# Re-ordering a fused attention and feed-forward kernel by a searched list, with its last up projection as seven block products

## The chip, the cores and the metric

The kernel runs on one core of a Trainium2 chip. The time is the device time of one execution in microseconds (us). Most executions of one kernel agree within a few tenths of a per cent. An execution is called slow when it is over 1.5% above the fastest of the same kernel. The engines are named as in the profile: PE is TensorE, PEld its weight loads, DVE is VectorE, ACT is ScalarE, POOL is GpSimd, and SP issues most transfers.

## The reference, cut to what matters

Four batches of eight heads with 768 tokens of width 64 go through an attention in which a token sees only the tokens of its own cluster. The result, 3072 tokens of width 512, goes through a feed-forward layer with exact GELU.

```
q_assign = argmax(q/|q| . c/|c|)          # 16 centroids per head; k the same
scores   = where(q_assign == k_assign, q @ k.T / 8, -1e9)
x        = (softmax(scores) @ v)          # -> (3072, 512)
h        = x @ w_in                       # 512 -> 2048, the "up projection"
out      = gelu(h) @ w_out                # 2048 -> 512, the "down projection"
```

## The kernel before

The kernel is a list of small operations. Each has an engine, an estimated duration, a due date, what it depends on and which buffers it takes. A greedy planner simulates the engines with assumed durations and orders the operations. The instructions of each engine then run in that order, so an engine whose next instruction has to wait stands, whatever is behind it.

```python
class Plan:
    def run(self):
        ...                                  # for each engine: the ready operation
        key = (t, op.due)                    # that can start first, then by due date
        ...
order = plan.run()
for op in order:
    op.emit()
```

The up projection of half a batch is 64 operations of two matmuls each, and eight full-width gelus:

```python
for m in (2 * half, 2 * half + 1):           # four of these per "hp" tile
    nc.tensor.matmul(T["hp", hb, fp][:, e, 0:QB],
                     w_in_sb[:, m, f * 128:(f + 1) * 128],
                     T["xt", b][:, m, t * QB:(t + 1) * QB],
                     start=(m == 0), stop=(m == NM - 1))
```

The down projection of a batch was already a 2x2 split with seven block products (of the Strassen-Winograd kind). It needs sums of the gelu outputs, called S1 to S4 here. Each is 128x768 in f16, there are 64 of them in the four batches, and all run on VectorE:

```python
def sums(k_, fs=fs):
    ...
    if k_ == 1:
        nc.vector.tensor_add(s1, a21, a22)
    else:
        sub(*{2: (s2, s1, a11), 3: (a21, a11, a21), 4: (a12, a12, s2)}[k_])   # nc.vector.tensor_sub
```

The k and q of a head are split into two f16 pieces, a tile called `st` of which three buffers exist. From head 8 on, `st` is transposed by a transfer (`dtr8`, `dtr9` and so on, tile `kqT`). TensorE then multiplies the result by the centroids, the "assignment" (`asn`).

The softmax here doesn't subtract the row's maximum and nothing guards it: scores larger than these inputs give would overflow.

Of the kernel before, what the change touches and what calls it, by code (L numbers as in the profile page):

```python
# [8 lines left out]
FP32 = mybir.dt.float32  # L9
# [10 lines left out]
    "0a 0b 1a 1b 2a 3a 4a 5a 2b 6a 7a 4b 5b 3b f0 6b 7b 8a 8b f1 9a 9b 10a 10b 11a "  # L20
# [5 lines left out]
SHIFT = dict((w.rsplit("=", 1)[0], int(w.rsplit("=", 1)[1])) for w in (  # L26
    "fc2_2_P6_0_1=41 fc2_0_P1_1_1=20 fc2_0_P2_0_1=18 fc2_0_P5_0_0=33 fc2_0_P5_0_1=6 "
    "fc2_0_P4_0_0=19 fc2_0_P3_0_1=21 fc2_0_P5_1_0=21 fc2_0_P7_1_1=23 fc2_0_P3_1_1=9 "
    "fc2_0_P4_1_0=21 fc2_0_P6_2_1=21 fc2_0_P5_2_1=21 fc2_0_P3_2_0=21 fc2_0_P4_2_0=33 "
    "fc2_1_P1_0_0=9 fc2_1_P2_1_0=33 fc2_1_P1_2_0=15 fc2_1_P6_0_0=23 fc2_1_P6_0_1=17 "  # L30
    "fc2_1_P7_0_0=9 fc2_1_P7_0_1=21 fc2_1_P5_0_0=14 fc2_1_P4_0_1=15 fc2_1_P6_1_0=22 "
    "fc2_1_P4_1_0=21 fc2_1_P6_2_1=24 fc2_1_P5_2_0=20 fc2_1_P5_2_1=22 fc2_1_P7_2_1=24 "
    "fc2_1_P3_2_0=35 fc2_1_P4_2_0=19 fc2_1_P4_2_1=16 fc2_2_P1_1_1=36 fc2_2_P2_1_1=-1 "
    "fc2_2_P1_2_0=18 fc2_2_P7_0_1=33 fc2_2_P4_0_0=33 fc2_2_P5_1_0=21 fc2_2_P7_1_1=21 "
    "fc2_2_P3_1_0=24 fc2_2_P3_1_1=6 fc2_2_P4_1_0=13 fc2_2_P6_2_1=18 fc2_2_P5_2_0=12 "
    "fc2_2_P7_2_1=21 fc2_2_P4_2_0=26 fc2_3_P1_0_0=21 fc2_3_P1_0_1=21 fc2_3_P1_1_0=23 "
    "fc2_3_P1_1_1=19 fc2_3_P5_0_1=22 fc2_3_P7_1_1=13 fc2_3_P3_2_1=21 fc1_4_0_3=-9 "
    "fc1_4_1_3=7 fc1_4_3_1=-9 fc1_6_6_3=-15 fc1_2_7_3=11 fc1_5_3_3=-2 fc1_6_3_2=-2 ge2=6 "
    "norm9_1=2 sc22a1=7 fc2_0_P1_2_0=18 fc2_0_P6_1_0=18 fc2_0_P6_2_0=18 fc2_0_P4_2_1=18 "
    "fc2_2_P1_1_0=18 fc2_2_P6_0_0=6 fc2_2_P5_0_0=27 fc2_3_P2_0_1=21 u30_3=-26 exp13b1=-64 "  # L40
    "exp13b2=-54 asnk30=-18 ge28=-1 S3_10=12 av29b1=17 exp12b1=-23 exp30b1=-36 exp2a2=14 "
    "exp4a1=26 exp2b0=17 exp2b2=26 exp5a0=29 exp5a1=19 exp6a0=-4 exp6a2=2 exp5b0=32 "
    "exp5b1=21 exp6b2=-11 sc4a2=27 evq0=10 fc1_0_1_3=24 fc1_0_7_0=-2 fc1_3_5_2=6 "
    "sc15a1=-8 sc15b0=-10 sc15b1=-9 dtr30=27 c221_0=-11 c221_3=-26 sc24a1=-20 sc24a2=-28 "
    "sc24b2=-21 ge27=-3 hik8=-3 stc1112=8 av6a0=42 av6a1=40 av6b0=41 loadv20=8 hik6=3 "
    "c211_1=11 fc2_0_P5_2_0=1 fc2_1_P1_0_1=-10 fc2_1_P1_1_1=9 fc2_1_P4_0_0=8 "
    "fc2_2_P6_1_0=1 fc2_2_P5_1_1=7 fc2_3_P7_2_1=1 gelu7_0=-3 sc2b0=-37 sc2b1=-38 "
    "sc2b2=-40 rec7_0=3 exp20b2=16 exp8a0=20 exp8b0=2 ohd24=2 putk7=8 evk1=5 t1_2=2 "
    "fold11=-5 fc1_0_6_0=13 fc1_5_7_2=13 fc1_6_5_3=19 av11a0=21 rec28_1=-11 sc29a2=-42 "
    "sc3b2=39 sc18a2=-10 v11=8 c110_1=-7 S2_32=-10 av10a2=10 av10b1=8 av10b2=-7 av11a1=20 "  # L50
    "av11b0=15 av12a1=10 av12a2=11 norm8_1=9 c222_1=16 c222_3=18 exp18a1=-39 exp18b2=-47 "
    "putk28=20 ohd16=11 gelu7_7=-2 ge31=-2 av2b1=23 exp22a0=5 exp22b0=11 exp23b2=-59 "
    "av7a0=47 exp31a2=14 asnq25=-11 loadv1=-4 u22_0=28 u22_1=26 u22_2=26 v17=14 ssq=3 "
    "exp24a1=-26 exp24b1=-30 exp25b1=-37 exp28a0=3 exp28b0=6 exp28b2=-14 rec3_1=-12 "
    "putk4=-15 gelu2_3=-10 av7a2=47 av7b2=45 putk15=-12 exp19a0=-33 exp19a2=-21 putq18=22 "
    "sc28a1=-20 exp11a0=-34 exp11a1=-34 exp12a1=-22 exp14a2=-72 exp14b0=-66 exp14b1=-64 "
    "exp15a0=-29 exp15b2=-24 exp16a1=-14 exp17a0=-1 ohd12=5 asnq19=-6 S4_00=10 loadq17=8 "
    "gelu0_4=30 gelu1_0=-3 gelu1_7=-12 gelu2_1=-34 gelu2_4=-20 gelu2_5=-25 gelu2_6=-8 "
    "gelu3_0=27 exp29a0=-16 exp29b0=-16 norm3_0=6 norm3_1=-10 S3_02=-13 sc28b0=-18 "
    "sc28b1=-17 u31_0=-23 exp17a2=1 av8a1=9 sc6b0=-16 p50_0=-17 p50_2=-4 p51_2=6 "  # L60
    "av15a1=-10 rec8_1=-3 fc1_6_4_0=-3 stc2211=-15 putq4=-11 hik24=6 hik26=6 stc1120=6 "
    "v1=-11 sc29b0=-27 c210_3=11 fc2_2_P1_0_1=5 asnk12=-1 sc0a2=-19 p11_3=-6 loadk27=-1 "
    "fev020=14 exp29a1=-37 exp28a1=-3 av27b1=-1 exp24a2=-29 amax11=-3 t2_3=-1 lok12=-3 "
    "av26b0=6 S3_20=2 hiq24=13 loadv18=-14 sc25a1=-18 stc2220=16 av31a0=-2 av31a2=7 "
    "av31b1=-7 av31b2=-15 sc9a0=-5 sc9a1=14 sc9b1=2 c120_1=-16 av16a0=22 p12_0=-17 "
    "p12_3=-15 asnk24=-1 asnk20=22 rec2_0=-10 amax17=-6 av3a0=51 av3a2=51 av3b2=51 "
    "hik14=-8 hik15=-8 exp12b2=-20 fin021=28 gelu7_3=1 exp1b2=-8 dtr13=-3 lok31=-25 "
    "norm6_0=15 norm7_0=1 norm12_1=-6 sc7b2=-5 av3b1=43 sc28a2=-12 sc28b2=-9 sc30a1=-12 "
    "sc30a2=-12 sc30b0=-12 sc30b1=-13 sc30b2=-24 v8=1 S4_22=2 av22b2=28 ge23=-3 v26=-16 "
    "av12b1=8 u31_2=-15 v10=10 av27b0=-2 sc6a1=-20 sc6b1=-13 rec15_1=1 fev130=-6 loq8=1 "  # L70
    "loadv29=-4 S1_12=-15 dfin10=4 av12a0=6 fin011=-5 hiq4=8 exp10a0=35 av7b0=51 av8a0=11 "
    "av8a2=5 av8b1=6 av8b2=7 av9a0=4 av9a1=4 sc10a1=-25 sc10b0=-32 sc10b1=-27 sc11a0=-9 "
    "sc11a1=-26 sc11b0=-27 sc14b1=7 sc14b2=6 evq3=-4 hiq16=-4 sc4a0=26 sc5a0=18 sc5a2=13 "
    "sc4b1=34 asnk9=6 asnk16=20 asnq15=-1 evq4=16 c120_2=-9 evk7=-3 asnk8=-13 stc1211=-29 "
    "hiq3=-1 loadk24=6 gelu1_3=13 gelu1_4=13 gelu4_0=40 gelu4_5=39 gelu6_1=12 gelu6_2=25 "
    "gelu6_3=12 gelu6_5=-1 fold16=-1 sc17a2=-4 sc17b0=-9 loadv28=8 hik30=8 av26a0=3 "
    "av28a1=16 av28a2=-16 loadv15=1 rec26_1=-4 S1_32=-19 sc16a0=-14 sc16a1=-12 sc16a2=-9 "
    "sc16b1=-2 loadk13=-8 av1b1=13 sc31b1=-10 sc31b2=-21 asnq5=2 asnq6=12 ge29=23 "
    "av23a2=-17 av23b2=-24 sc7a0=-15 sc7b1=1 exp12a2=-21 ohtr1=-6 u20_3=-13 rec7_1=-21 "
    "ohtr4=-6 asnk31=-1 ge6=-27 asnk25=5 exp11b0=-16 rec17_1=-5 exp16b2=-9 gelu0_3=52 "  # L80
    "asnq10=12 loadv22=-5 loadv23=-10 loadv24=-15 putq10=7 putq12=-3 putq13=6 amax18=5 "
    "S4_13=1 loadq6=-5 amax19=-7 exp7b2=16 exp3b0=-12 fc1_4_1_1=-2 fc1_1_1_2=-2 loadq2=-1 "
    "putq8=-3 loq31=2 c121_3=-33 rec0_0=-8 c211_3=28 sc2a1=-35 fc1_0_5_1=-4 hik27=15 "
    "fc1_7_5_2=-11 exp26b0=3 sc19a1=-9 ohd20=-10 fin230=2 loq24=20 putq23=-5 putq9=-8 "
    "u32_1=17 trk0=3 ge8=2 exp14a1=-53 exp15b1=-10 amax4=-8 fc2_1_P2_0_1=1 exp30a1=-23 "
    "fc1_4_6_0=6 putk20=1 putk22=17 fc1_0_4_3=10 exp17a1=7 exp17b1=1 exp20a2=-5 "
    "exp22b2=36 exp30a0=-11 exp31b2=6 amax1=-7 evq1=8 ge11=-5 loadk5=7 sc23a0=-7 "
    "sc23a2=-6 sc23b1=-7 fc1_0_3_2=-4 fc1_0_4_1=-3 fc1_2_0_3=-30 fc1_2_5_2=16 "
    "fc1_2_6_0=-5 fc1_2_6_1=-13 fc1_3_4_0=11 fc1_3_5_0=7 fc1_3_7_0=7 fc1_4_0_1=-13 "
    "fc1_4_2_2=-22 fc1_4_4_2=-3 fc1_4_4_3=-6 fc1_4_7_0=-7 fc1_5_5_3=-24 fc1_5_6_0=20 "  # L90
    "fc1_6_3_1=20 fc1_6_6_0=-14 fc1_7_0_0=14 fc1_7_0_1=-3 putk31=3 sc3a0=34 sc3a2=36 "
    "exp3a0=7 exp3a2=-1 exp5a2=13 exp3b1=-4 loq16=-19 gelu6_7=15 stc2120=5 sc0a1=1 "
    "sc8a0=-5 sc8b1=-5 sc8b2=-8 loadq8=-12 av25a1=11 ge22=-15 stc2213=5 av24b0=-6 "
    "c111_3=5 fold23=17 hiq26=8 S3_21=3 rec22_1=22 norm20_1=-4 norm21_1=9 S4_10=13 "
    "S3_30=3 fc2_0_P2_1_1=2 fc2_0_P2_2_1=1 fc2_0_P7_0_0=13 fc2_0_P5_1_1=8 fc2_1_P1_2_1=-5 "
    "fc2_1_P6_1_1=-2 fc2_2_P1_0_0=8 fc2_2_P5_0_1=2 fc2_2_P4_0_1=-8 fc2_2_P6_2_0=8 "
    "fc2_3_P1_2_0=-5 fc2_3_P4_2_1=12 gelu0_1=17 gelu0_2=32 gelu0_7=34 fin130=12 "
    "sc25b1=-12 sc25b2=-12 sc9a2=-3 sc9b0=-3 sc9b2=-9 av13a2=-8 putk12=-14 av0b0=-4 "
    "exp29a2=-21 av30b2=12 amax16=5 S4_31=-2 av23a0=-6 t4_0=13 dtr12=4 asnq26=-12 "
    "sc17b1=13 S2_03=-2 gelu7_4=33 lok30=-6 exp28b1=8 loadq15=-22 norm15_1=4 sc5b2=4 "  # L100
    "sc8a2=-10 sc11b1=-13 lok27=-5 t3_1=-9 cn=-13 ohd26=9 ohd28=1 ohd30=-6 norm5_0=18 "
    "asnk3=-17 v29=-21 stc1220=11 putk3=3 hiq23=6 hiq27=12 hiq29=9 hiq30=24 S3_33=34 "
    "exp23a0=-42 exp23b0=-38 stc2221=-16 trq5=1 exp3b2=-15 sc27b1=-1 sc27b2=-18 amax2=3 "
# [150 lines left out]
class Slot:  # L254
# [3 lines left out]
    def __init__(self, pool):  # L258
        self.pool, self.users, self.place = pool, [], None
# [974 lines left out]
```

## Time and profile before

| | before |
|---|---|
| time, median of 3 runs (lowest to highest) | 302.88 us (301.42 to 303.34) |
| span of the profiled run | 301.1 us |
| first score product, first up projection | 13.95, 51.78 us |
| start of the last two up projections | 257.83 us |
| 128x768 f16 sum on VectorE, mean of each of its four groups | 563 to 622 ns |

The prediction shows the totals, the stages and the dear groups. The list of waits of TensorE has in its columns who waited, for what, how many us in all, how many times, and the longest:

```profile
PE sc_ps L844 <- ACT p_sb L853: 2.8, 7, 0.6
PE sc_ps L844 <- DVE kqT L791: 1.6, 3, 0.7
PE warm_ps L436 <- DVE half L465: 1.5, 1, 1.5
PE x_ps L881 <- DVE x_tok L908: 1.1, 3, 0.4
PE op L1125 <- DVE S L1015: 0.8, 1, 0.8
```

In the whole run TensorE stands 1.2 us for sums of the down projection (0.8 in the last line, and 0.4 in a line of the same kind, for tile `g`, that is not shown). These are the groups on VectorE that will change or, just as tellingly, not change (busy us in all, mean ns of one):

```profile
L703 DVE TENSOR_REDUCE asb<-asn_ps 128x192 f32<-128x384 f32 x24 | 13.3, 555 | 13.1 <-PE asn_ps L687 12.9
...
L791 DVE TENSOR_SCALAR kqT<-ohT 16x768 f16<-16x768 f16 x24 | 11.6, 482 | 7.6 <-DMA ohT<-oh 7.1
...
L1015 DVE TENSOR_TENSOR S<-S,g 128x768 f16<-128x768 f16 x16 | 9.1, 570 | 0.3
L1051 DVE TENSOR_TENSOR S<-g 128x768 f16<-128x768 f16 x16 | 9.0, 563 | 27.4 <-ACT g L997 27.4
...
L718 DVE TENSOR_REDUCE amax<-asb 128x12 f32<-128x192 f32 x24 | 8.4, 351 | 0.6
```

And the first transposes of `st` by transfer, issued between 30 and 60 us, from issue to landing:

```profile
DMA to landing us min/median/max: 3.8/4.4/6.2
```

### The profile page before, as it was taken

The numbers are of one execution on the slowest core, as the hardware profiler recorded it, in microseconds if no ns is written. First come the engines' busy times: TensorE is split into PE (matmuls) and PEld (weight loads), VectorE is DVE, ScalarE is ACT, GpSimd is POOL, SyncE is SP. The second block draws the span as 40 slices with busy tenths as digits, with TensorE's granted clock in tenths as the row PEclk, the third lists the DMA queues.
The fourth block names the chain that finished last, engine by engine and source line by source line (L and its number), as shares of the span: only waits on it lengthen the run. The fifth ranks groups of instructions, "written<-read, shape, count | busy, mean of one in ns | idle before, by whom it ended". The sixth has DMA issues, their size and how long they took to land.

```text
span 301.1 us, 8247 instructions
## 1 busy us (share of the span) xinstructions
PE 287.6 (96%) x3388; PEld 212.5 (71%) x3388; DVE 186.4 (62%) x432; ACT 216.3 (72%) x278; POOL 120.6 (40%) x192
## 2 busy tenths in 40 slices
PE   7899878999989999999999999999999999999995
PEld 3577655677657878866677787866678788656874
DVE  3479879966598665752676866762556553206663
ACT  5488699679689988986689778976589998366100
POOL 6989529866521976484005826620000000000020
PEclk9999999999999999999999999999999999999999
DMA  7999995998849998989229969811027312100123
GB/s 258 308 241 239 291 204 135 201 221 160 222 126 134 230 217 195 244 194 254 80 39 196 175 148 212 141 45 27 0 63 123 89 31 70 53 2 0 37 70 106
DMA packets 78038, 43.50 MB, mean 144 GB/s; under 512 B 57008, under 2 KB 77488, under 8 KB 78000
## 3 DMA queue, kind: packets, MB, share of 16 engines
q1 hardware_dynamic: 75024, 38.55, 55.7%
q0 software_dynamic: 2688, 4.19, 7.8%
q8 instruction: 26, 0.43, 0.6%
q10 hardware_dynamic: 288, 0.23, 0.2%
q14 instruction: 12, 0.10, 0.1%
HBM read 27.30 MB, written 6.29 MB: 112 GB/s over the span
## 4 chain that ended last, share of the span: by engine, by line
PE 81%; DVE 10%; ACT 5%; issue 1%; DMA 1%; POOL 0%; ACTq 0%; DVEq 0%
PE hp L983 25%; PE op L1125 22%; PE sc_ps L844 17%; PE x_ps L881 10%; ACT p_sb L853 5%; PE asn_ps L687 2%; DVE g L1015 2%; DVE kqT L791 2%; DVE kqT L788 1%; PE tr_ps L642 1%; DMA cent_sb<-in_centroids_dram 1%; PE both_ps L642 1%; DVE S L1015 1%; DVE S L1051 1%; PE warm_ps L436 1%
## 5 line engine op out<-in xcount | busy, mean ns | idle before, releaser
L853 ACT ACTIVATE p_sb<-sc_ps 128x768 f16<-128x768 f32 x192 | 146.5, 809 | 20.9 <-PE sc_ps L844 18.1
L844 PE MATMUL sc_ps<-kqT 80*128 80x384 f16 x384 | 92.3, 325 | 4.6 <-ACT p_sb L853 2.8
L983 PE MATMUL hp<-xt,w_in_sb 128*128 128x384 f16 x512 | 85.9, 326 | 0.0
L997 ACT ACTIVATE g<-hp 128x768 f16<-128x768 f32 x64 | 51.8, 811 | 35.4 <-PE hp L983 35.2
L983 PEld LDWEIGHTS <-w_in_sb 128*128 128x128 f16 x512 | 49.2, 98 | 31.4 <-issue 0.3
L881 PEld LDWEIGHTS <-p_sb 128*128 128x128 f16 x1152 | 47.7, 97 | 12.8 <-PE sc_ps L844 1.5
L881 PE MATMUL x_ps<-vaug,p_sb 128*128 128x65 f16 x1152 | 52.0, 193 | 1.1 <-DVE x_tok L908 1.1
L1125 PEld LDWEIGHTS <-g 128*128 128x128 f16 x480 | 45.1, 97 | 10.9 <-DVE g L1015 0.8
L1179 POOL TENSOR_TENSOR c<-u,p 128x256 f32<-128x256 f32 x12 | 9.4, 787 | 107.8 <-DVE p L1163 67.9
L844 PEld LDWEIGHTS <-kqT 80*128 80x128 f16 x384 | 32.1, 98 | 11.7 <-issue 4.8
L1125 PE MATMUL op<-w_out_sb,g 128*128 128x256 f16 x288 | 38.7, 272 | 0.4 <-DVE g L1015 0.4
L597 POOL CAST vaug<-v_raw 128x384 f16<-128x384 f32 x32 | 16.8, 534 | 46.3 <-PE x_ps L881 45.0
L583 POOL TENSOR_TENSOR st<-q_raw,st 128x384 f16<-128x384 f32 x31 | 29.1, 943 | 1.7
L583 POOL TENSOR_TENSOR st<-k_raw,st 128x384 f16<-128x384 f32 x31 | 28.9, 934 | 2.0 <-ACT st L444 0.8
L1125 PE MATMUL op<-w_st,g 128*128 128x256 f16 x192 | 27.2, 272 | 0.0
L1051 DVE TENSOR_TENSOR S<-g 128x768 f16<-128x768 f16 x16 | 9.0, 563 | 27.4 <-ACT g L997 27.4
L1125 PEld LDWEIGHTS <-S 128*128 128x128 f16 x192 | 17.8, 97 | 5.6 <-DVE S L1015 1.1
L703 DVE TENSOR_REDUCE asb<-asn_ps 128x192 f32<-128x384 f32 x24 | 13.3, 555 | 13.1 <-PE asn_ps L687 12.9
L446 POOL CAST st<-k_raw 128x384 f16<-128x384 f32 x29 | 15.3, 530 | 14.7 <-DMA kqT<-st 13.4
L908 DVE TENSOR_TENSOR x_tok<-x_ps,rec 128x384 f16<-128x384 f32 (+1 forms) x40 | 19.1, 477 | 1.3
L901 DVE RECIPROCAL rec<-x_ps 128x6 f32<-128x6 f32 (+1 forms) x40 | 7.5, 186 | 16.7 <-PE x_ps L881 16.2
L446 POOL CAST st<-q_raw 128x384 f16<-128x384 f32 x29 | 16.3, 564 | 3.1 <-DMA q_raw<-in_q_dram 3.1
(81 smaller groups left out, 283.7 us busy)
## 6 DMA issues: line engine op xcount, KB each, us to landing
q_raw<-in_q_dram SPq DMA_DIRECT2D x32, 192.0 KB, 4.1
v_raw<-in_v_dram SPq DMA_DIRECT2D x32, 192.0 KB, 4.0
out_dram<-c SPq DMA_DIRECT2D x48, 128.0 KB, 2.0
k_raw<-in_k_dram SPq DMA_DIRECT2D x31, 192.0 KB, 3.8
w_in_sb<-in_moe_w_in_dram POOLq DMA_DIRECT2D x4, 512.0 KB, 8.0
w_out_sb<-in_moe_w_out_dram POOLq DMA_DIRECT2D x4, 512.0 KB, 12.0
kqT<-st SPq DMA_TRANSPOSE x24, 4.5
k_raw<-in_k_dram ACTq DMA_DIRECT2D x1, 192.0 KB, 3.6
```

Source lines behind the costliest of these rows:

```text
L446: engine[eng].tensor_copy(o, i)
L583: engine[eng_lo[w]].tensor_sub(t[:, :, D:2 * D], T[w + "raw", i], t[:, :, 0:D])
L597: nc.gpsimd.tensor_copy(vaugs[turn("va", i)][:, :, 0:D], T["vraw", i])
L703: nc.vector.tensor_reduce(out=T["asb", i], in_=T["asn", i].rearrange("p n w (a c) -> p n w c a", a=2), axis=AX.X, op=ALU.add)
L844: nc.tensor.matmul(s_ps[:, e, 0:QB], T["kT", i][0:D + C, c * 128:(c + 1) * 128], T["qT", i][0:D + C, t * QB:(t + 1) * QB], start=True, sto ...
L853: nc.scalar.activation(T["p", i, t][:, 2 * cp:2 * cp + 2, :], T["sc", i, t, cp][:, :, 0:QB], ACT_FN.Exp, bias=0.0, scale=float(scale))
L881: nc.tensor.matmul(o, T["p", i, t][:, ch, jj * 128:(jj + 1) * 128], vaugs[turn("va", i)][:, ch, 0:D + 1], start=(ch == 0), stop=(ch == N - 1))
L908: nc.vector.tensor_tensor(T["xtok", b][:, h // 2, j0:j0 + nn, h % 2 * D:(h % 2 + 1) * D], T["x", key][:, :, 0:D], T["rec", key].to_broadca ...
L983: nc.tensor.matmul(T["hp", hb, fp][:, e, 0:QB], w_in_sb[:, m, f * 128:(f + 1) * 128], T["xt", b][:, m, t * QB:(t + 1) * QB], start=(m == 0 ...
L997: nc.scalar.activation(T["g", hb][:, :, fp, :], T["hp", hb, fp][:, :, 0:QB], ACT_FN.Gelu, bias=0.0, scale=1.0)
L1051: nc.vector.tensor_add(s1, a21, a22)
L1125: nc.tensor.matmul(T["op", b, key], a()[:, f, j * 128:(j + 1) * 128], w[:, f, :], start=(start and f == 0), stop=(f == NB - 1), skip_group ...
```

## The change

The intent is less TensorE work in the last up projection, which nothing else can hide, and a tighter order everywhere. The greedy planner goes. In its place stands a fixed list of operation names, found by a search over list orders, and a word may name another engine than the default. In that list, 30 of the 64 S sums and 23 weight and token sums go to GpSimd. In return many casts and residuals of the splits go from GpSimd to VectorE and ScalarE, and some copies from VectorE to ScalarE.

```diff
-    def run(self):                          # greedy choice by assumed times
+    def run(self, table):                   # the list decides; dependencies are asserted
+        for word in table:
+            name, _, eng = word.partition("@")
+            ...
+            op.emit(*([eng or op.eng] if op.alt else []))
...
+TABLE = (
+    "dm ones cent zero2 ident loadq0 loadk0 ssq exptab hik0 zero3 hiq0@POOL loq0 loadk3 "
...
-                    nc.vector.tensor_add(s1, a21, a22)
+                    engine[eng].tensor_add(s1, a(1, 0), a(1, 1))
...                                          # last batch: seven products per feature block
+        elif e[1] < 2 * B - 2:
             make_fc1(e[1])
+    make_fc1_sums(pos["f", 2 * B - 3] + 20)  # 16 sums of w_in blocks
+    make_fc1_blocks(B - 1)                   # 8 x 7 x 2 = 112 matmuls instead of 128
...
+            def prod(p, key, start, deps, take=(), at=0.0, fp=fp, a=a, due=due):
+                    for m in range(2):
+                        nc.tensor.matmul(o, a[p](m), r[p](m), start=start and m == 0, ...)
...
-    dm = const.tile([128, 512], FP16, name="dm")     # dummies: 19 of 384 columns
+    dm = const.tile([128, 640], FP16, name="dm")     # 10 of 512 and 8 of 128
-    W_AT = (1, 2, 3, 4, 5, 6, 7, 7)                  # when the weights are loaded
+    W_AT = (1, 2, 2, 3, 3, 4, 5, 5)
```

The new block takes its PSUM and SBUF from pools of the attention, which are released when the attention no longer needs them. `w_in` is loaded by column blocks instead of row blocks, and 12 more transposes of x become transfers.

## The prediction

> **What bounds the kernel now.** I read the engine totals first, then busy time by stage, then the groups of instructions, then the chain of waits and the timelines at both ends. The page opens with this row:
>
> ```profile
> PE 287.6 (96%) x3388; PEld 212.5 (71%) x3388; DVE 186.4 (62%) x432; ACT 216.3 (72%) x278; POOL 120.6 (40%) x192
> ```
>
> TensorE is busy 96% of the span, so only two things can pay: less TensorE work, or less time in which it waits or does no useful work. Where the latter lies shows in the windows view, cut at the first score product (13.95 us), the first up projection (51.78), the last two up projections (258.0 to 278.8) and the end. The columns are the stretch, its length, busy us of PE, PEld, DVE, ACT and POOL, granted clock, DMA share, GB/s.
>
> ```profile
> 0.00:13.95 13.95, 10.43 (x98) 6.41 (x99) 5.76 (x18) 6.44 (x13) 11.16 (x31) 1.00 0.89 285
> 13.95:51.78 37.83, 33.19 (x574) 25.06 (x574) 32.23 (x79) 31.02 (x42) 26.89 (x42) 1.00 0.96 223
> 51.78:258.00 206.22, 204.51 (x2423) 152.40 (x2423) 130.78 (x299) 165.89 (x208) 80.15 (x118) 1.00 0.67 141
> 258.00:278.80 20.80, 20.80 (x130) 12.58 (x129) 5.18 (x10) 12.16 (x15) 0.00 (x0) 1.00 0.06 20
> 278.80:301.10 22.30, 18.67 (x168) 16.01 (x166) 12.45 (x28) 0.81 (x1) 2.42 (x3) 0.99 0.21 72
> ```
>
> From 51.78 to 297.9 TensorE is dense, with about 2 us idle. Ahead of that it is not: in the second stretch ACT and DVE are each 82 to 85% busy beside a TensorE at 88%, and in the first one TensorE is mostly waiting or running dummies. The costs of single instructions come from these groups (busy us in all, mean ns, then idle before and its releaser):
>
> ```profile
> L853 ACT ACTIVATE p_sb<-sc_ps 128x768 f16<-128x768 f32 x192 | 146.5, 809 | 20.9 <-PE sc_ps L844 18.1
> L844 PE MATMUL sc_ps<-kqT 80*128 80x384 f16 x384 | 92.3, 325 | 4.6 <-ACT p_sb L853 2.8 <-DVE kqT L791 1.6
> L983 PE MATMUL hp<-xt,w_in_sb 128*128 128x384 f16 x512 | 85.9, 326 | 0.0
> L1163 DVE COPY p<-op 128x256 f32<-128x256 f32 x12 | 5.1, 425 | 6.6 <-PE op L1125 6.6
> ```
>
> The mean ns of a matmul includes its drain, so I use pitches from the chain of waits: 128 up-projection products take 20.80 us, 0.1625 each; eight down-projection ones 0.875, 0.109 each; a score pair 0.33; an attention-value six 0.18; six transposes 0.34 warm. Back-to-back exponentials take 10.58 us for 14 on the timeline, 0.756 each.
>
> The two chain lines that explain the start: twelve transposes at 107 ns each early, six at 57 ns later.
>
> ```profile
> 6.85 1.29 PE both_ps L642 x12
> ...
> 14.44 0.34 PE tr_ps L642 x6
> ```
>
> **What the Trainium skill says.** (1) "TensorE: Matmul & The Clock Gate", Part 1: a cold array runs at half rate, N/1.2 ns per matmul, and about 3.4 us of sustained activity release it. The 107 and 57 ns above agree; the dummies before 4.84 us also go at 0.338 us for 384 columns, and the release comes only at about 11 us, after several pauses. The granted clock on the page (1.00) doesn't show this gate. (2) "PSUM — Partial Sum Buffer", "The four PSUM rules": one matmul output stays within one bank of 512 FP32. A 128x384 f32 bank tile of the new block therefore takes a whole bank, and three tags by two buffers take six, just those that the score, attention and transpose pools give back; nothing in the trace of before tests it. (3) "VectorE: DVE Perf Modes", "Why PSUM operands drop a tier": FP32 read from PSUM goes at one element per cycle. The 128x256 copy at 425 ns agrees (267 ns of it streaming at 0.96 GHz). (4) "GPSIMD Engine Reference", Specifications: GpSimd shares SBUF interfaces with VectorE, with contention on instructions with two SBUF inputs. The trace agrees: at 287.5 us one 128x768 subtraction takes 1083 ns beside a GpSimd addition, against a median of 550.
>
> **The change, part by part.** I counted instructions and their order in the built kernel; durations are those above.
>
> *Last up projection.* It replaces 128 products of 384 columns by 7 x 2 x 8 = 112. TensorE: 16 x 0.1625 = -2.6 us. It adds work on the other engines: per feature block two half-width gelus, one full gelu, three copies, two additions. As ordered, ACT gets 16 half gelus, 11 copies and 8 full gelus; DVE 29 operations. A 128x384 f32 operation is not in the trace. I estimate 0.55 us on DVE (425 + 128/0.96 ns), and on ACT 809 - 384/1.2 = 0.49, or about 0.41 in pitch. In sum ACT 27 x 0.41 + 8 x 0.73 = 17 us, DVE 29 x 0.49 = 14 us plus some operand sums for the down projection, against TensorE's 112 x 0.1625 = 18.2. So TensorE stays the bound by a hair, but the block is now a chain. One feature block holds its second bank from the copy to the last gelu: copy 0.5, product 0.5, copy 0.6, product 0.5, addition 0.6, product 0.5, gelu 0.5 = 3.7 us, two buffers, so 1.85 us per block against 2.28 of TensorE. That is only 0.4 us of slack in an in-order queue. I allow 0.9 us of stalls: **-1.7 us** net. Its operand sums (16 on the weights, 8 on the tokens) lie where DVE and GpSimd have room: DVE is 63% busy in the third stretch.
>
> *Start.* The order now transposes head 0's q alone, copies k and q through two separate banks, runs both assignments together and makes the first one-hot sooner. Before, the second assignment sat behind twelve transposes of head 1 (8.79 to 10.36 us), and the two puts waited for a 0.80 us copy on ACT (12.52 to 13.35). By hand: q lands at about 4.4, cast and residual to 5.7, centroid chain to 7.0, k transposed 7.7, copied 8.4, assignments 8.9, maximum and compare 9.7, one-hot transposed 10.3, two puts 11.5, scores at 12.0 against 13.95. **-2.0 us.** The wide dummies (10 of 512 and 8 of 128 columns for 19 of 384) matter through the clock alone; half of 24 cold transposes would be 1.2 us and is partly in this chain.
>
> *13.95 to 51.78.* TensorE's useful work by pitch: 42 score pairs 13.9, 39 sixes 7.1, 72 transposes 4.1, 24 more 1.4, 144 assignment products 3.6, 15 final transposes 0.9: 31 of 37.8 us. So 6.9 us are lost there. The other bounds, after: ACT 41 x 0.756 + 1.8 of moved copies = 33 us; DVE, counted from the new order, 72 operations of about 28 us against 79 of 32.2. The floor is ACT's 33 us, 4.8 below today. A global order should reach part of it: **-2.8 us**, a choice of somewhat over half.
>
> *51.78 to 258.* Twelve final transposes become DMA transposes (12 x 0.057 = -0.7). Idle was 1.7 us; flexible placement should find some, while 30 down-projection sums moved to GpSimd at an estimated 1.9 us (787 ns for 128x256, scaled to 128x768 at about 2.45 ns per column as in the 943 ns rows) may slow DVE: **-0.9 us.**
>
> *Down projection and tail.* 168 products of 0.109 = 18.4 us remain; the one wait of 0.39 us at 288.6 may go; the last addition and store, 3.2 us after the last product, stay: **-0.2 us.**
>
> Sum: -2.0 - 2.8 - 0.9 - 1.7 - 0.2 = -7.6, so 302.9 - 7.6 = 295.3.
>
> **The rivals.** *A: the block turns into a chain.* If each of its eight steps waits only 0.4 us longer than I allow, 3.2 us are lost, the product saving is gone, and the time is 298.5. For it: the small slack, and ACT at 17 of 18.2 us. Against: the first products of the down projection can fill, and the order interleaves two feature blocks. *B: the order is worth nothing on the chip.* A search works on assumed durations and arrival times; the old order was tuned too. Then only the TensorE savings of 2.6 + 0.7 remain, less stalls, and the time is about 301. For it: the old middle is already dense. Against: the first 52 us are not, and the losses there come from in-order queues. *C: contention.* GpSimd's 30 sums and DVE's new splits slow each other; at 0.5 us on each of 30 DVE neighbours this is 15 us of DVE time, mostly hidden, and perhaps 2 us on the path: 297. *D: all goes well*, with the second stretch at ACT's floor: 291 to 292.
>
> **Range and chances.** A 2% gain needs 296.8. My estimate is 1.5 us below that, and the four uncertain terms are each good to 1.5 us or so. That gives 290.5 to 300 for eight in ten, 0.63 for faster, 0.35 for within 2%, 0.02 for slower.
>
> **What would show each step.** First score product at 12.0 us (start); first up projection at about 47 us, with ACT's exponentials nearly back to back (second stretch); from the first seven-product matmul to the first down-projection product of that batch 19 to 20 us with under 1.5 us of TensorE idle (block); no idle of note between; a tail of 3.2 us after the last product. The prediction is wrong if the first up projection is no earlier than 50 us, if TensorE's idle in the block exceeds 3 us behind copies on ACT and DVE, or if DVE's 128x768 sums beside GpSimd's stretch far above 0.55 us and TensorE waits for them.

## The result, and the profile after

The changed kernel is slower: 326.50 us (median of 4 runs, 324.35 to 329.17) against 302.84 (4 runs). The ratio is 1.079, with a 95% interval of 1.070 to 1.089. Here and below, a ratio is the mean time of one kernel's fast runs over that of the other's fast runs of the same rounds, so it is not quite the ratio of the medians. The output is correct.

This is the changed kernel's page, the row of engine totals:

```profile
PE 291.9 (91%) x3359; PEld 213.8 (66%) x3359; DVE 230.5 (71%) x472; ACT 234.5 (73%) x326; POOL 156.7 (49%) x174
```

TensorE has 29 matmuls fewer and yet is busy 4.3 us longer. It is also idle 30.6 us of a span of 322.5, where it was idle 13.5. The windows view, cut at the first score product, the first up projection, twice where it gets worse, at the block and at the end, tells where (columns as in the prediction):

```profile
13.17:49.50 36.33, 32.93 (x540) 24.75 (x540) 29.99 (x72) 30.18 (x42) 27.33 (x39) 0.95 1.03 217
49.50:80.00 30.50, 29.77 (x310) 20.66 (x309) 18.98 (x44) 26.11 (x35) 16.65 (x18) 1.00 0.95 199
80.00:105.00 25.00, 17.21 (x179) 11.56 (x177) 24.63 (x36) 13.60 (x17) 20.05 (x16) 0.86 0.44 106
105.00:280.30 175.30, 164.65 (x1943) 122.44 (x1941) 118.08 (x246) 136.28 (x178) 67.55 (x65) 0.98 0.59 125
280.30:319.60 39.30, 37.02 (x282) 27.21 (x279) 29.86 (x59) 21.21 (x42) 14.77 (x10) 1.00 0.13 42
```

The start and the second stretch are shorter than before (36.3 against 37.8 us), and so is the last stage (39.1 against 40.0 us from the first matmul of the last up projection to the end of the last one of the down projection; the window above ends 0.2 us later). What was lost lies between 49.5 and 280.3 us: 230.8 us, against 206.05 before. In the third line VectorE is busy 24.63 of 25 us, GpSimd 20.05, and TensorE only 17.21, at a granted clock of 0.86. TensorE's list of waits says what it stands for:

```profile
PE op L1227 <- DVE S L942: 6.9, 3, 3.8
PE x_ps L809 <- DVE x_tok L836: 6.3, 3, 3.8
PE op L1227 <- DVE p L382: 3.0, 3, 1.5
PE op L1227 <- DVE u L1264: 2.7, 1, 2.7
PE asn_ps L618 <- DMA kqT<-st: 1.6, 2, 0.9
```

The first four lines are all VectorE, 18.9 us. So why is VectorE late? Its groups in the changed kernel:

```profile
L726 DVE TENSOR_SCALAR kqT<-ohT 16x768 f16<-16x768 f16 x23 | 15.3, 667 | 6.3 <-DMA ohT<-oh 5.8
...
L634 DVE TENSOR_REDUCE asb<-asn_ps 128x192 f32<-128x384 f32 x24 | 13.3, 552 | 15.2 <-PE asn_ps L618 15.2
...
L1147 DVE TENSOR_TENSOR S<-g 128x768 f16<-128x768 f16 x11 | 9.8, 895 | 5.8 <-ACT g L925 5.8
...
L942 DVE TENSOR_TENSOR S<-S,g 128x768 f16<-128x768 f16 x8 | 8.5, 1068 | 0.1
L649 DVE TENSOR_REDUCE amax<-asb 128x12 f32<-128x192 f32 x24 | 8.4, 348 | 0.4
...
L942 POOL TENSOR_TENSOR g<-g,S 128x768 f16<-128x768 f16 x10 | 17.8, 1786 | 9.1 <-PE op L1227 9.1
```

Two groups of sums of two SBUF tensors went from 563 and 570 to 895 and 1068 ns (the other two, not shown, from 598 and 622 to 931 and 730), and the TENSOR_SCALAR form from 482 to 667. The reductions did not move, neither the one that reads PSUM (555 to 552) nor the one that reads SBUF (351 to 348). VectorE is not slower in general: some kinds of instruction are, now and then. The last line is GpSimd's largest group of such sums, 1786 ns each. The timeline shows when. GpSimd and then VectorE, from 82 to 97 us (start, duration):

```profile
82.44 1.95 POOL L942 TENSOR_TENSOR g<-g,S 128x768 f16<-128x768 f16 x1
...
85.13 1.74 POOL L942 TENSOR_TENSOR g<-g 128x768 f16<-128x768 f16 x1
...
94.72 1.75 POOL L942 TENSOR_TENSOR g<-g,S 128x768 f16<-128x768 f16 x1
```

```profile
82.81 1.99 DVE L1147 TENSOR_TENSOR S<-g 128x768 f16<-128x768 f16 x1
...
85.30 1.98 DVE L942 TENSOR_TENSOR S<-S,g 128x768 f16<-128x768 f16 x1
...
91.18 0.56 DVE L942 TENSOR_TENSOR S<-S,g 128x768 f16<-128x768 f16 x1
...
94.98 1.90 DVE L942 TENSOR_TENSOR g<-g 128x768 f16<-128x768 f16 x1
```

Add start and duration. GpSimd's sums end at 84.39, 86.87 and 96.47. The VectorE sums that began beside them end at 84.80, 87.28 and 96.88, each 0.41 us later. The one at 91.18 has no GpSimd sum beside it and takes 0.56 us. That is not two engines sharing a road: VectorE stands until GpSimd's instruction is over and then does most of its work (0.41 of the 0.56 us). It is no accident of three rows. In the traces of all 18 kernels of this document, 92 VectorE sums of this shape take over 0.8 us, and every one of them ends 0.40 to 0.43 us after a GpSimd instruction. Nor need that instruction be a sum: in the kernel before, one takes 1.27 us from 83.56 us on beside the residual of a split, and one 0.81 us from 82.83 us on beside a cast. "SBUF — State Buffer", section "Who interferes with whom", of the Trainium skill states just this: the port pair that the two share is an exclusive lock held for the whole instruction, taken on VectorE's side by an instruction with two SBUF inputs or in a two-port mode, and a TENSOR_REDUCE on this chip never contends. The groups above agree with it line by line. The prediction had read only the page on GpSimd, which says that there is contention and not of what kind.

### The profile page after: what moved, and what is told of

Same layout as the page of the kernel before. It is cut to its first block, busy times and chain, and to the rows that moved or that the text cites. A ratio compares the mean times of both kernels' runs of the same rounds, so it can differ in the third digit from the quotient of the medians.

```text
span 322.5 us, 8292 instructions
## 1 busy us (share of the span) xinstructions
PE 291.9 (91%) x3359; PEld 213.8 (66%) x3359; DVE 230.5 (71%) x472; ACT 234.5 (73%) x326; POOL 156.7 (49%) x174
## 4 chain that ended last, share of the span: by engine, by line
PE 65%; DVE 26%; DMA 4%; issue 3%; ACT 1%; POOL 0%; DVEq 0%
PE op L1227 17%; PE sc_ps L777 15%; PE hp L912 12%; PE x_ps L809 9%; PE fx_ps L1048 6%; DVE kqT L726 3%; DVE S L942 3%; DVE S L1147 2%; DVE kqT L717 2%; DVE oh L655 2%; DMA kqT<-st 2%; DVE st L382 2%; DVE st L521 2%; PE asn_ps L618 2%; DVE vaug L382 2%
## 5 line engine op out<-in xcount | busy, mean ns | idle before, releaser
L912 PE MATMUL hp<-xt,w_in_sb 128*128 128x384 f16 x384 | 65.9, 326 | 0.0
L912 PEld LDWEIGHTS <-w_in_sb 128*128 128x128 f16 x384 | 36.5, 98 | 23.2 <-issue 0.8
L925 ACT ACTIVATE g<-hp 128x768 f16<-128x768 f32 x48 | 38.9, 810 | 15.2 <-PE hp L912 14.2
L521 POOL TENSOR_TENSOR st<-k_raw,st 128x384 f16<-128x384 f32 x21 | 19.9, 951 | 14.4 <-ACT st L380 11.8
L942 POOL TENSOR_TENSOR g<-g 128x768 f16<-128x768 f16 x7 | 13.1, 1871 | 23.4 <-ACT g L925 19.3
L634 DVE TENSOR_REDUCE asb<-asn_ps 128x192 f32<-128x384 f32 x24 | 13.3, 552 | 15.2 <-PE asn_ps L618 15.2
L521 POOL TENSOR_TENSOR st<-q_raw,st 128x384 f16<-128x384 f32 x21 | 19.9, 952 | 5.6 <-DVE st L382 5.1
L942 POOL TENSOR_TENSOR g<-g,S 128x768 f16<-128x768 f16 x10 | 17.8, 1786 | 9.1 <-PE op L1227 9.1
L382 POOL CAST st<-q_raw 128x384 f16<-128x384 f32 x19 | 10.7, 561 | 23.2 <-DMA kqT<-st 11.4
L1227 PE MATMUL op<-w_st,S 128*128 128x256 f16 x96 | 14.9, 281 | 7.4 <-DVE S L942 6.9
L829 DVE RECIPROCAL rec<-x_ps 128x6 f32<-128x6 f32 (+1 forms) x40 | 7.5, 187 | 19.7 <-PE x_ps L809 19.2
L726 DVE TENSOR_SCALAR kqT<-ohT 16x768 f16<-16x768 f16 x23 | 15.3, 667 | 6.3 <-DMA ohT<-oh 5.8
```

The source lines that it names most:

```text
L382: engine[eng].tensor_copy(o, i)
L521: engine[eng].tensor_sub(t[:, :, D:2 * D], T[w + "raw", i], t[:, :, 0:D])
L726: nc.vector.tensor_scalar(dst, src, float(VAL), None, op0=ALU.mult)
L912: nc.tensor.matmul(T["hp", hb, fp][:, e, 0:QB], w_in_sb[:, m, f * 128:(f + 1) * 128], T["xt", b][:, m, t * QB:(t + 1) * QB], start=(m == 0 ...
L925: nc.scalar.activation(T["g", hb][:, :, fp, :], T["hp", hb, fp][:, :, 0:QB], ACT_FN.Gelu, bias=0.0, scale=1.0)
L942: engine[eng].tensor_sub(o, a, c)
```

## The experiments

All kernels gave a correct result; there is no e11 and no e13 on record. The times are medians; "before" is the kernel before in the same rounds on the same chip.

| run | us | before | ratio (95%) |
|---|---|---|---|
| e1 changed, 30 S sums on VectorE | 310.42 | 302.60 | 1.027 (1.024 to 1.030) |
| e2 e1, and all other sums on VectorE | 309.81 | 302.60 | 1.021 (1.016 to 1.027) |
| e3 before, the same 30 S sums on GpSimd | 306.39 | 302.60 | 1.015 (1.010 to 1.019) |
| e4 e1, and 30 sums on GpSimd that nobody needs | 331.88 | 302.60 | 1.095 (1.089 to 1.101) |
| e5 e2, assignment of heads 8 and 9 later | 309.12 | 302.64 | 1.021 (1.018 to 1.025) |
| e6 e5 with the old last up projection | 310.75 | 302.64 | 1.027 (1.024 to 1.030) |
| e7 e5 with 384-column dummies | 310.17 | 302.64 | 1.017 (1.011 to 1.022) |
| e8 e2 with earlier weight loads | 308.50 | 302.28 | 1.021 (1.018 to 1.025) |
| e9 e5 with earlier weight loads | 313.17 | 302.28 | 1.036 (1.033 to 1.039) |
| e10 changed, earlier weight loads | 327.98 | 302.28 | 1.088 (1.082 to 1.093) |
| e12 old order, new block | 300.01 | 302.62 | 0.992 (0.990 to 0.994) |
| e14 e9 with four `st` buffers | 309.06 | 302.62 | 1.024 (1.020 to 1.028) |
| e15 e14, transposes issued later | 308.31 | 302.62 | 1.020 (1.017 to 1.024) |
| e16 e8 with four `st` buffers | 307.17 | 302.62 | 1.015 (1.013 to 1.017) |
| e17 e12 with later weight loads | 304.33 | 302.86 | 1.005 (0.998 to 1.012) |
| e18 e12 with four `st` buffers | 300.24 | 302.86 | 0.991 (0.986 to 0.996) |

### The sums on GpSimd (e1 to e4)

The theory is that GpSimd's sums stop VectorE. One rival: they are only slow (1.75 us and more where VectorE takes 0.56), and what needs their results comes late. Another: the order itself is bad. e1 and e2 take the sums off GpSimd and leave the order of the list alone.

```diff
-    "... S4_00@POOL ... S3_03@POOL ..."        # 30 such words
+    "... S4_00 ... S3_03 ..."
```

> The changed kernel with its 30 activation sums of 128x768 (the S operations) put back from GpSimd to VectorE, order unchanged; 23 weight and token sums stay on GpSimd. Theory 1 (GpSimd and VectorE exclude each other on two-input SBUF operations, so each 1.8 us sum on GpSimd stops VectorE): VectorE busy time falls from 230 us towards 205 although 30 operations are added to it, its 128x768 sums fall from about 0.9-1.07 us to about 0.6, the time falls to 304-312. Theory 2 (the new order itself is bad, the queues wait for each other): the time stays above 320. Theory 3 (the sums merely come late because GpSimd takes 1.8 us for each): time also 304-312, so this run alone does not separate it from theory 1; e4 does.

> As e1, and the 23 weight and token sums put back to VectorE too; only residual splits, casts and a few f32 additions stay on GpSimd. Theory 1: another 3-8 us less than e1, 299-305 us, the early down projection (80-105 us of the trace) free of PE waits over 1 us. Theory 2: above 318. If neither, and the time is between 306 and 316, the order has a share of its own.

e1 took back 16 of the 24 us that were lost. Its row of engine totals:

```profile
PE 288.6 (94%) x3359; PEld 210.3 (68%) x3359; DVE 209.1 (68%) x502; ACT 234.2 (76%) x326; POOL 103.0 (33%) x144
```

VectorE got 30 sums more and became 21.4 us less busy. Thirty sums at about 0.63 us (e1's own rows say 601 to 657) are 19 us, so in the changed kernel each GpSimd sum had cost VectorE (21.4 + 19) / 30 = 1.3 us of standing, 40 us in all. By kind of instruction, from e1 to the changed kernel, only about half of the 40 us lies on two-input instructions, sums and residuals. The 61 TENSOR_SCALARs take 10.2 us more, and the 35 casts, most of which the change itself had moved to VectorE, 7.9 us more; the TENSOR_REDUCEs and the copies out of PSUM take the same. e2, with the other 23 sums moved too, is hardly further, 309.8, where 3 to 8 us were expected: by its own third case the order has a share too. Its profiled run was one of the slow ones, so I read no size from it.

e3 does the opposite, in the old order:

```diff
+ON_POOL = set("S4_00 S3_03 S3_02 ... S4_32".split())          # the same 30
+                e = nc.gpsimd if f"S{k_}_{b}{fs.start // 2}" in ON_POOL else nc.vector
-                    nc.vector.tensor_add(s1, a21, a22)
+                    e.tensor_add(s1, a21, a22)
```

> The kernel before with the same 30 of its 64 activation sums emitted on GpSimd, everything else and the order unchanged. Theory 1 and 3: 312-322 us, VectorE busy time up although it has 30 operations fewer, remaining VectorE sums well above 0.6 us. Theory 2: 302-306 us.

It loses 4 us, well short of the 312 to 322 us that the theory had expected. The standing is there (two groups of the VectorE sums left have means of 909 and 932 ns instead of 563 and 570, the other two go from 622 to 834 and from 598 to 555), but there is less of it: VectorE's busy time falls by 5.7 us (186.4 to 180.7) where 30 sums of about 0.59 us are 18, so a GpSimd sum costs VectorE 0.4 us here against 1.3 in the changed kernel. The old order also has 1 cast on VectorE instead of 35. So the same 30 sums cost 4 us in one order and 16 in the other, and in the old one they met less of VectorE's work.

e4 tells the theory of the lock from the rival of late results. It is e1, with 30 more sums on GpSimd on a private tile that nobody ever reads.

```diff
+    junk = const.tile([128, 2, QB], FP16, name="junk")
+    plan.busy = lambda: nc.gpsimd.tensor_sub(junk, junk, junk)
-    "... S4_00@POOL ..."
+    "... S4_00 busy ..."
```

> As e1, the 30 sums on VectorE, and at each place where one of them stood on GpSimd a sum of the same shape and type on a private tile that nobody reads. Theory 1 (exclusion): as slow as the changed kernel or slower, 318-335 us, VectorE's two-input SBUF operations again stretched, PSUM-reading ones at 0.42 and 0.55 us as before. Theory 3 (only the late results hurt): within 3 us of e1.

No one waits for those sums, and yet the kernel goes from 310.4 to 331.9 us. That kills the rival. Another one, that the dummies delay GpSimd's own casts and residuals, finds nothing in the waits: TensorE, VectorE and ScalarE together wait for GpSimd 0.8 us in e4 and 1.2 us in e1, and TensorE waits less for the transposes of `st` (1.8 us against 6.6). These are e4's groups, the dummy sums first:

```profile
L379 POOL TENSOR_TENSOR junk<-junk 128x768 f16<-128x768 f16 x30 | 47.5, 1583 | 1.4
```

```profile
L948 DVE TENSOR_TENSOR g<-g 128x768 f16<-128x768 f16 x16 | 15.0, 951 | 0.6 <-ACT g L931 0.6
...
L640 DVE TENSOR_REDUCE asb<-asn_ps 128x192 f32<-128x384 f32 x24 | 13.3, 553 | 15.5 <-PE asn_ps L624 15.5
...
L655 DVE TENSOR_REDUCE amax<-asb 128x12 f32<-128x192 f32 x24 | 8.4, 348 | 0.4
```

The group of VectorE's sums that is hit hardest stretches to 951 ns (all four have 654 to 951, against 601 to 657 in e1), and the reductions keep their 553 and 348. VectorE is busy 238.6 us against 209.1, about 1 us more per dummy. It is the running of a GpSimd sum itself that costs.

### The 7 us that are left (e5, e8, e9, e10)

With the sums on VectorE the changed order is still 7 us behind. In e1's list of waits the first line is another one now:

```profile
PE asn_ps L616 <- DMA kqT<-st: 6.6, 3, 4.3
PE x_ps L807 <- DVE x_tok L834: 2.5, 2, 1.6
```

The search's list has the first transposes of `st` by transfer, and the assignments behind them, earlier than the old order. e5 moves the assignments of heads 8 and 9 and what hangs on them behind a later gelu. e8 moves three weight loads forward, so that they are out of the way. e9 does both, and e10 is the changed kernel, GpSimd sums and all, with the weights of e8.

```diff
 # e5
-"... asnk9 asnq9 ... fold9 amax9 ... asnk8 asnq8 fold8 amax8 ... ge9 ge8 ohd8 putk9 ... gelu0_4 ..."
+"... gelu0_4 asnk9 asnq9 fold9 amax9 asnk8 asnq8 fold8 amax8 ge9 ge8 ohd8 putk9 ..."
 # e8
+"... w2 w1 ... w3 w6 w4 ..."     # and away from their later places
```

> e2 (all f16 sums on VectorE) with the cluster assignments of heads 8 and 9, the first two whose operands come by DMA transpose, moved some 24 up-projection pieces later in the order, with the VectorE steps that follow from them. Theory: in e1 and e2 TensorE stood 4.3 and 7.4 us behind these two (waiting for the DMA transpose), and ran at half clock for some us after; moved later, both go: 298-302 us. Rival (the order is slow in many small places, and the wait just moves to the next instruction that needs the transposes or the one-hots): 305-309 us.

> e2 (all f16 sums on VectorE) with the last three of the eight weight loads (the second block of w_in, the third and first of w_out) issued right after the loads ahead of them, at some 24 to 31 us instead of 40 to 50. Theory: the first DMA transposes, which in e2 and e5 shared the DMA engines with these loads and took up to 16 us to land against at most 6.2 in the kernel before, land within 7 us; TensorE's 7.4 us wait near 50 us and the half clock after it go; 297-302 us. Rival (the early loads of k, q and v are delayed instead, by as much): 305-310 us.

> e8 with the assignments of heads 8 and 9 moved later, as in e5. If the transposes land in time after e8's edit, moving the assignments is needless: within 1.5 us of e8. If they still land late, 1 to 4 us faster than e8.

> The changed kernel itself with the weight loads early, its sums still on GpSimd. If exclusion between GpSimd and VectorE is the larger cause and acts later (80 to 260 us), the time stays at 318-325 us; if the late transposes were most of it, below 312.

The theories of e5, e8 and e9 missed, and e5 and e8 ended about where their rivals had put them. e5 is the same as e2: the wait did not go but moved, to 1.9 us on a reduction of VectorE and 2.6 us on the transposes of the next heads. e8 gained nothing that the ratios show (1.021 as for e2): the first up projection starts at 46.5 us, and then TensorE stands 5.7 us at the assignment all the same. e9 is worse than both. There the splits of heads 10 and 11 stood at the head of the queues of ScalarE and GpSimd, waiting for one of the three `st` buffers, which the late transposes still held. e10 shows that the weights do not touch the larger cause: 328.0, on the side that was expected and 3 us above the range.

### The block and the dummies (e6, e7)

e6 is e5 with the last up projection as it was; e7 is e5 with sixteen dummies of 384 columns.

```diff
-        elif e[1] < 2 * B - 2:
+        else:
             make_fc1(e[1])
-    make_fc1_sums(pos["f", 2 * B - 3] + 20)
-    make_fc1_blocks(B - 1)
```

> e5 with the last up projection undone: 128 plain products, one gelu of 128x768 per pair as in the kernel before; no weight or token sums for it, early pools kept. Theory that the seven products save what the prediction said (1.7 us net of stalls): 1 to 3 us slower than e5. Rival that their copies, additions and operand sums cost as much as they save: equal to e5 within 0.8 us, or faster.

> e5 with dummies of 384 columns (16 of them, the same 6144 columns in all) in place of ten of 512 and eight of 128. If the width matters through the clock gate: first transposes slower and the first score product 0.5-1.5 us later, the time 0.5-1.5 us longer. Rival: no difference beyond the spread of 0.5%.

e6 is 1.6 us slower than e5 in the same rounds, so the seven products are worth 1.6 us. e7 against e5 shows no effect beyond its own spread (307.1 to 313.0, with one slow run): inconclusive, and too small to matter here.

### The old order with the new block (e12), and the rest of the order (e14 to e18)

e12 takes the sequence in which the old planner had emitted its operations and writes it down as the list, engines included, up to the last up projection. From there on it takes the new block. The 16 weight sums go to VectorE in the batch before. The rest of the change (wide dummies, 12 more transposes as transfers) stays out.

> The order of the kernel before up to its last up projection, with all its sums and splits on the engines they had there; only the last up projection is the seven block products of the change, with its 16 weight sums on VectorE in the idle places of the batch before and its 8 token sums just ahead of the block. Theory (the change lost by its new order and its engines alone, the block itself is worth 1.6 to 2 us): 300.5 to 301.5 us, ratio 0.993 to 0.997, block and last down projection about 38 us. Rival (the late pools and the 24 added sums cost as much as the products save, and e5 against e6 only showed it in a disturbed order): 302 to 304 us.

It gives 300.0 us and beats both kernels: 0.992 of the kernel before, which is clear of the noise but under 2%. In its windows view, from the first up projection to the block, through the block (to just before the first down projection product, after which a few of the 112 matmuls still come), and through the down projection:

```profile
49.70:255.80 206.10, 204.42 (x2423) 152.35 (x2422) 135.91 (x316) 164.57 (x207) 80.14 (x118) 1.00 0.66 141
255.80:273.66 17.86, 17.40 (x107) 10.17 (x105) 16.43 (x38) 15.54 (x30) 0.00 (x0) 1.00 0.07 23
273.66:293.84 20.18, 19.96 (x177) 16.91 (x175) 14.78 (x34) 5.88 (x12) 0.00 (x0) 1.00 0.18 59
```

The middle is 206.1 us, as before the change (206.05), and the last stage 38.2 us against 40.0. The new block, with both other engines 87 to 92% busy in it, costs TensorE 0.46 us of idle time in 17.86.

The changed order with all sums on VectorE should come near this, but it does not. Three runs look at the transposes and the buffers that they hold, one at a time: four `st` buffers instead of three (e14 on e9, e16 on e8), and transposes issued behind more loads (e15).

```diff
-    POOLS = {"raw": 4, "st": 3, ...
+    POOLS = {"raw": 4, "st": 4, ...            # e14, e15, e16, e18
-"... dtr8 ... dtr9 ... loadv13 ..."
+"... loadv13 dtr8 dtr9 ..."                    # e15
```

> e9 (all sums on VectorE, early weights, assignment of heads 8 and 9 later) with four instead of three buffers for the split pieces. Theory (in e9 the late transposes of heads 8 and 9 hold the split buffers, so the splits of the heads behind them block ScalarE and GpSimd, and the transposes of heads 10 and 11 come late in turn): waits of e9 for p_sb (2.3 us) and for the transposes at 70 us (4.1 us) shrink, 313 falls to about 306. Rival (the waits come from the saturated transfers alone): within 1 us of 313.

> e14 with the transfers that transpose heads 8 and 9 also issued later, behind the loads that are ahead of them in the kernel before. Theory (transposes issued while the loads fill the queues land late): they land within 6 us of their issue, the assignment no longer stands, 2 us below e14 or more. Rival (late is late: the assignment stands on them as long as before, because they are only issued later): same as e14 or slower.

> e8 (all sums on VectorE, early weights, the changed order otherwise) with four split buffers. Theory of the split buffers: the 5.7 us wait for transposes at 53.7 us stays, since the first two heads do not wait for a buffer, and what follows is freer: 306 to 308 us against 308.5. Rival: 308.5 unchanged.

The fourth buffer gives 4 us to e9 and 1.3 us (by the ratios 1.9) to e8, in rounds on different chips. This agrees with the theory that late transposes hold the buffers and so stop the splits, for a part: e9's wait of 2.3 us behind ScalarE is gone in e14, the one of 4.1 us for transposes is not. e15 is no faster than e14 beyond the spread. Its transposes take less time from issue to landing (6.1 to 11.3 us against 8.6 to 13.4), but they land no earlier (52.4 and 53.8 us against 51.7 and 53.5), and TensorE waits 4.2 us, until 64.9 us, for the transposes of the next heads: late is late.

e16 is the best of the changed order, and its account nearly closes, though no run took its remaining wait away. Its TensorE is busy 286.2 us and idle 18.9 of 305.1; in e12 it is busy 284.4 and idle 13.0 of 297.4. So of the 7.7 us between the two spans, 5.9 are idle time and 1.8 slower matmuls. Its list of waits, first line, and the landing of its first transposes:

```profile
PE asn_ps L615 <- DMA kqT<-st: 6.8, 2, 5.5
```

```profile
DMA to landing us min/median/max: 9.4/11.8/14.2
```

e12 has no wait for these transposes. The 6.8 us are then the idle time, and the half clock after it makes the slower matmuls. e16's windows around the wait, with the granted clock third from the end:

```profile
48.00:52.00 4.00, 0.00 (x0) 0.00 (x0) 0.00 (x0) 0.92 (x2) 0.00 (x0) 0.69 1.25 230
52.00:56.00 4.00, 3.65 (x49) 2.64 (x50) 1.42 (x3) 0.00 (x0) 0.50 (x1) 0.50 0.53 174
```

TensorE does nothing for 4 us and afterwards runs at half its clock for as long again. In the first of these lines the transfer engines are full (DMA share 1.25). That suggests the reason for the late landing: e16's transposes, issued at 36.3 and 42.9 us while loads fill the queues, take 14.2 and 9.4 us, and those of the kernel before, issued from 49.5 us on, take 6.2 at most. e17 tests one side of it, by moving the four loads of `w_in` in e12 to later places. e18 is e12 with four buffers.

> e12 (old order, new block; 300.0 us) with one thing moved: the four loads of the first weight matrix are issued later, about where the changed order has them (the last one at about 42 us instead of 21 us), so that they are under way when the transposes of heads 8 and 9 are issued at 47.5 us. Theory (a transpose that is issued while weight loads fill the queues lands late, and TensorE then stands at the assignment): the first transposes land 9 us or more after issue instead of 5.3 at most, TensorE waits some us there, 303 to 306 us. Rival (the transposes of the changed order are late for another reason, the weights do not matter): landing within 6 us and 300 us as e12.

> e12 with four split buffers instead of three. In the old order no wait of TensorE on a transpose is left in the profile of e12, so the theory of the split buffers expects nothing: 300.0 us within 1 us. Rival (the buffers are worth 2 to 4 us in any order, as e14 and e16 suggest): 297 to 298.5 us.

e17's time came out in the range that the theory named, and still the theory fell, for the late landing that it asked for was missing. The transposes issued in that stretch landed within 4.5 us, and TensorE waited for none of them. It stood instead 1.8 us, until 50.4 us, for an attention result of VectorE (a `fin_ps` product behind `x_tok`), and ran at half clock from 32.7 to 39.5 us and from 49.8 to 56.6. Late loads of `w_in` cost some 4 us, but not through the transposes. e18 is the same as e12: a fourth buffer helps only where transposes are late. What makes the transposes of the changed order late stays open. The time of issue alone does not: the changed kernel's first two, issued at 38.6 and 42.5 us, land after 4.1 and 7.3 us, e2's (39.3 and 42.2) after 4.3 and 15.5. In e8, e9, e10, e14, e15 and e16, the runs with early weights, the first two land between 49.9 and 54.6 us whenever they were issued (36.3 to 47.7). The loads of `w_in` alone, in the old order, do not do it. The loads of q, k and v, which the changed list also has earlier, were not tried.

## Why the prediction was wrong

The prediction was 295.3 us (290.5 to 300) and faster; measured were 326.5.

*The step that failed* is "51.78 to 258", put at -0.9 us, with its sentence that 30 sums moved to GpSimd "may slow DVE". From the first up projection to the last one it measured 230.8 against 206.05 us, **+24.7**. About half of that is GpSimd's: from the first score product to the last up projection the changed kernel needs 267.1 us, e1 256.1 and the kernel before 243.9. The other half is the order's own loss, where the step had hoped that "flexible placement should find some" of the idle time. The mechanism was named, in this step, in rival C and among the signs that would prove the prediction wrong. Its size was wrong in two terms. Rival C took "0.5 us on each of 30 DVE neighbours"; e1 against the changed kernel shows 1.3 us per GpSimd sum, on casts and TENSOR_SCALARs as well as on sums. And it took the result as "mostly hidden, and perhaps 2 us on the path"; e1 against the changed kernel shows 16. The first error came from one row (1083 ns against 550), read as two engines that slow each other, when it was one engine that stands until the other is done (that row, too, ends 0.42 us after the GpSimd addition beside it). GpSimd's sum takes 1.75 to 1.87 us, so the neighbour loses up to that. The second came from VectorE's 63% share over 206 us. A share over a long stretch says nothing about the 25 us in which VectorE, splits and sums together, is 98% busy and stands between TensorE and its next operand. And busy time includes the standing: from 80 to 105 us VectorE gets 36 instructions done in 24.63 us in the changed kernel, and 51 in 23.56 us in e1.

*A cost that the prediction did not have at all* is what TensorE pays after a wait. Without GpSimd's sums, in the old order, and with the same saving, TensorE is busy 284.4 us (e12). In the changed kernel it is busy 291.9 us: 7.5 us more for 13 matmuls fewer. Most of that is the clock. The record of the granted clock has four stretches at half (20.8 to 24.2, 89.1 to 95.9, 106.2 to 109.6 and 249.5 to 252.9 us), in which TensorE works for 13.9 us, so some 7 us are lost; e12 has none from its first score product to its last matmul. "TensorE: Matmul & The Clock Gate", Part 1, of the Trainium skill says that an idle window of about 3.4 us takes the clock back to half, and the prediction used that page only for the start. The runs agree on the half (0.50 after 4 us of nothing in e16), but not that it takes so long a pause: half clock follows pauses of 1.29 us (the changed kernel at 17.5 us), 1.84 us (e17 at 48.6 us) and 2.69 us (the changed kernel at 101.9 us), and does not follow one of 2.12 us (at 303.7 us). Here the measurements decide. The prediction's remark that the granted clock on the page does not show the gate holds for the start of the kernel before only; here it does show it.

*The start*, -2.0 us: not resolved. The first score product came at 13.17 us, not 12.0; in the other changed orders with the same dummies it came between 11.5 and 13.5. But it came at 11.9 and 13.3 us in e12 and e18, which share one start, and at 13.95 and 12.7 in the two profiles of the old start (before and e3). The spread from run to run is as large as the step. A reading was wrong, too: between the two assignments at 8.79 and 10.36 us the trace has six transposes and two dummies, not twelve transposes.

*13.95 to 51.78*, -2.8 us: this measured -1.5 in the changed kernel. In the old order the stretch is 37.8 us in every profile (before, e3, e12, e18) but e17's, with its late loads. In the changed order with the sums on VectorE it is 32.4 us in e1, 33.4 in e16 and up to 36.1 in the others (e9), so the step's floor of 33 us was about reached, in the best of them. But the up projection started early with other work left undone behind it, and the transposes took the gain back. From the first score product to the last up projection the old order needs 243.9 us (before and e12) and the changed one 252.3 (e16) or 256.1 (e1).

*The block*, -1.7 us net: right. e6 minus e5 gives 1.6, e12's last stage 1.8. It did not turn into a chain (rival A). In the changed kernel TensorE has no gap in the 19.2 us from the block's start to near its end, as the prediction's test asked (the first down-projection product comes earlier than asked, after 17.2 us), and in e12 it idles 0.46 us. ScalarE at 15.5 us in e12's block stands beside the estimate of 17.

*Down projection and tail*, -0.2 us: small in size, but with a new wait of 2.1 us for a sum in the changed kernel. It belongs to the failed step.

*Rival B* (the order is worth nothing, 301 us) was the nearest to what can be had: e12 is the old order with the block and gives 300.0. The search's order is worth less than nothing on the chip, even in the best form that was tried: 307.2 with all sums on VectorE, early weights and a fourth buffer.

## What to carry to other kernels

Before moving two-input work to an engine that looks idle, ask which instructions of the neighbour lock with it, and count the neighbour's loss as up to the whole length of the moved instruction (1.3 us on the average here, and 0.4 in an order where the two rarely met); a dummy instruction that nobody needs (e4) measures it in one run. Judge an engine by its busiest 25 us, not by its average, and look for half clock after each wait of TensorE over a microsecond; it came after many of them, not after all. And take a large change apart: the one part with a sure saving, put into the old order, was the only version that beat the kernel before (e12, and e18 with one more buffer).

## What the Trainium skill lacked or had wrong

- "GPSIMD Engine Reference", Specifications and Key points: it calls it contention with VectorE instructions of two kinds, without saying that it is an exclusive lock, which stands only in "SBUF — State Buffer", Who interferes with whom. A reader of the first page alone, as I was, sizes it as a slowdown. Measured: a VectorE sum of 0.56 us took 1.90 to 1.99 us, and 1.3 us of VectorE time were lost per GpSimd sum on the average.
- "GPSIMD Engine Reference", Key points: VectorE is said to be about twice as fast on elementwise work. For a 128x768 f16 sum it was 0.56 us against 1.75 to 1.87 in the changed kernel and 1.58 in e4, about three times.
- "SBUF — State Buffer", Who interferes with whom: right in each kind that these runs show (sums of two SBUF tensors and TENSOR_SCALAR stretch, TENSOR_REDUCE keeps 348 to 351 ns). It gives no idea of the cost in a whole kernel: the same 30 sums cost 4 us in one order (e3) and 16 in another (e1 against the changed kernel).
- "TensorE: Matmul & The Clock Gate", Part 1: says that the array goes cold after at least one idle window of about 3.4 us. Here half clock, for 3.4 or 6.8 us, also followed pauses of 1.29, 1.84 and 2.69 us.
- No page I read tells how long a transpose by transfer takes beside a full load: 3.8 to 6.2 us from issue to landing in the kernel before, 9.4 to 14.2 in e16, for the same tile.
